# Fused sigmoid attention and low-rank mixing FFN on one core: six pairs' q and k loaded at once, float32 results emptied by VectorE, a new set of planner numbers

## The chip, the cores and the metric

The kernel runs on one core of a Trainium2 chip. The metric is the device time of one execution in microseconds; the median of three runs before the change is 1539.1 us (1538.2 to 1541.37). The engines are named as in the profile: PE (TensorE, matmuls), DVE (VectorE), ACT (ScalarE), POOL (GpSimd) and SP (SyncE, whose queue issues every DMA here).

## The reference, cut to what matters

```python
# q, k, v: (8 batches, 12 heads, 448, 64) float32
scores = q @ k.transpose(0, 1, 3, 2) / sqrt(64) - log(448)
x = (1 / (1 + exp(-scores))) @ v            # -> (8, 448, 768)
xt = x.transpose(0, 2, 1)
u = x + (xt @ U @ V).transpose(0, 2, 1)     # U (448, 32), V (32, 448)
out = u + maximum(u @ w1, 0) @ w2           # w1 (768, 3072), w2 (3072, 768)
```

The weights come to the device as the int64 bits of float64 numbers; the kernel decodes them to float32 itself and splits them into a high and a low float16 part.

## The kernel before, in words

Work is cut by batch. Heads go in pairs (six pairs p in a batch b); two neighbouring pairs, an even and an odd one, form a quad, because the last 64 of 448 rows of both are done together. For each pair `loads` fetches q, k and v, `scores_of` makes scores on PE (L547, and L551 for the last rows), ACT takes the sigmoid (L664), `values_of` multiplies with v (L566, L576), and `out_of` (L703) empties the PSUM bank into one of the six tiles ua or ub of the batch. Batches 0 and 1 (`WHOLE = 2`) do this in float32. The later ones split everything into float16 parts first (the tiles stg, made by POOL and DVE) and their results are scaled when they leave PSUM.

`mix` then does the U and V product for a batch: transposes on PE (L752), copies by ACT (L763), a product with U (L764), a copy (L781), a product with V (L790), an addition by DVE (L792), and `u_parts` splits the result into the float16 tiles us (us__87 for batch 0, us__88 for batch 1). Batch 0 is mixed in two halves, of three tiles each.

The FFN of batches 0 to 3 runs in six groups of w1 and w2 (`ffn_in`, L938; `ffn_out`, L958). In batch 0 each group is decoded on the way: `decode` loads four pieces of int64 bits by SP into one of three w tiles, DVE and ACT turn them into float32 (L401, L404; L453), ACT finds a bound of each piece (L464) and empties the w tile by it, PE spreads the maximum over the partitions (L420), and then the high part (ACT, L908) and the low part (DVE, L404, for example w__90<-stg,s_w__178,w__90) are written and the group is stored in DRAM (kept). Batches 4 to 7 take a form with seven instead of eight products (L1146) from about 958 us on.

The order of the instructions is not written by hand. Every instruction is recorded with an engine, a cost and a place (a number that says how early it is wanted); `Plan.order` then walks a model of the engines and, of the instructions that are ready, issues the one with the least place. The numbers at the top of the file (L59 to L69) set places and the model's costs. Tiles are handed out by the same walk: a ring of buffers has a queue, and a load can be issued when a buffer of its ring is free. The engines run their own lists strictly in order, SP's list of DMA issues too.

Rings that matter here: qk has three buffers (qk__99 to qk__101) for q and k of a pair, v has four (v__102 to v__105). H are the two tiles of the FFN's inner activations (h__93, h__94), unused until the first `ffn_in` of batch 0. The load of q and k is four DMAs of 64 rows for a pair, since each head lies in half of the partitions.

Of the kernel before, what the change touches and what calls it, by code (L numbers as in the profile page):

```python
# [38 lines left out]
P = 128  # L39
D = 64  # L40
# [15 lines left out]
LATER = [2, 4, 3, 5, 6, 7]  # L56
FORMS = {1: (0,), 2: (1,), 3: (2,)}
MM = 0.1893
SWITCH, BOND = 0.11, 6.183  # L59
PIPE, LANDS, LATE = 0.33e6, 3.237, 0.546  # L60

ROOM0, ROOM, AHEAD, BEFORE, PACE = -7.852, 308.311, -53.442, 95.466, 1.111
PREP, BOUNDS, VALUES, SECOND, MIXED = 19.918, -15.21, 0.731, 3.0, 3.524
MIXED1, MIX_1 = 6.837, -10.814
MIX_2, EV_IN, EV_OUT, A_OFF = 34.703, 70.659, 39.745, -7.081
START, DECODE = 63.04, 64.674
U_AT, U_STEP = -3.425, 6.242
LEAD, SUMS, STEP_K, STEP_I, FFN_LEAD = -5.194, 216.012, 10.066, 62.433, 60.97
W_AT, W_STEP, PAIR0, MIX0A, MIX0B, W2_LAG, G0_LEAD = -69.485, 11.668, 3.029, -290.85, -260.87, 0.576, -7.653  # L69
LOW_G = 1  # L70
FB, AB = 8, 0
SHIFT = dict()
# [162 lines left out]
def fused_kernel(ctx: ExitStack, tc: tile.TileContext, q, k, v, wu, wv, w1, w2, out):  # L235
# [12 lines left out]
    def ring(name, n, shape, dtype):  # L248
        return [Buffer(buf(f"{name}{i}_", shape, dtype)) for i in range(n)]
# [194 lines left out]
    def to_f32(words, t, kw, kt, pos, low=False):  # L444

        def lo():
            return words()[:, :, 0]

        def hi():
            return words()[:, :, 1]  # L450

        if low:
            act(0.84, lambda: nc.scalar.activation(  # L453
                t().bitcast(F32), words().bitcast(U16)[:, :, 1], AF.Identity, bias=minus2, scale=-0.936 * 2.0 ** -35), [kw, "minus2"], [kt], pos)
            dve2(0.97, lambda: stt(t(), hi(), 3, t(), ALU.logical_shift_left, ALU.bitwise_or), [kw, kt], [kt], pos)
# [64 lines left out]

    def loads(b, p, early):
        plan.group = f"L{b}{p}"
        qk, v32 = plan.tile("qk", QK), plan.tile("v", V32)
        for h in range(2):
            for i, src in ((1, k), (0, q)):
                load(lambda i=i, h=h: qk.x[rows_of(h), i, :], lambda src=src, h=h: src[b, p, rows_of(h), h, :],
                     D * S * 4, [], [(qk, i, h)], early, cost=0.62)
        load(lambda: v32.x, lambda: v[b, p], P * 512 * 4, [], [(v32, 0), (v32, 1)], early + 0.1)
        mine, other = rows_of(p % 2), rows_of(1 - p % 2)
        load(lambda: v32.x[mine, 3, other], lambda: v[b, p, other, 3, other], D * D * 4, [], [(v32, 1)], early + 0.2)  # L530
        return qk, v32, [(qk, i, h) for i in range(2) for h in range(2)]

    quads = {}

# [48 lines left out]
    def pair(b, p, at, d):  # L583
# [8 lines left out]
        if whole:  # L592
            c, kc = 1.0 / math.sqrt(D), []

            def score_products():
                return [(qk.x[:, 1, :], qk.x[:, 0, :])]

            def value_products():
                return [(v32.x, lambda t, h: t.x[:, h * S : (h + 1) * S])]

            def last_products():
                return [(v32.x[:, 3], lambda t, h: t.x[:, h * S : (h + 1) * S])]

            kscore, kvalue, klast = kqk, [(v32, 0)], [(v32, 1)]
        else:
            prep = at - PREP
            st, sv, ss = plan.tile("stq", STQ), plan.tile("stv", STV), sm("ss", 3)
            v3 = quads[b]["v3"] if odd else plan.tile("v3", V3)
            cm = quads[b]["cm"] if odd else sm("cm", 1)
            mine = rows_of(p % 2)  # L610
            for i in range(2):
                bound(lambda i=i: qk.x[:, i, :], S, lambda i=i: ss.x[:, i : i + 1], kqk[2 * i : 2 * i + 2], (ss, i), prep - BOUNDS, 0.68)
            bound(lambda: v32.x.rearrange("p a b -> p (a b)"), 512, lambda: ss.x[:, 2:3], [(v32, 0), (v32, 1)], (ss, 2), prep - BOUNDS, 0.73)
            s, inv = scale_by_dma(ss, [(ss, i) for i in range(3)], 3, "qkv", prep - BOUNDS + 1)
            cc, cv = sm("c", 1), sm("cv", 1)
            pool(0.3, lambda: ts(nc.gpsimd, cc.x, inv.x[:, 0:1], inv.x[:, 1:2], ALU.mult, 1.0 / math.sqrt(D), ALU.mult), [inv], [cc], prep + 1)
            pool(0.2, lambda: ts(nc.gpsimd, cv.x, inv.x[:, 2:3], 1.0 / A_UP, ALU.mult, 1.0, ALU.mult), [inv], [cv], prep + 1)
            pool(0.2, lambda: ts(nc.gpsimd, cm.x[mine], cc.x[mine], 1.0, ALU.mult, 1.0, ALU.mult), [cc], [(cm, odd)], prep + 1)

            def part(n):  # L620

                n = (2, 3, 1, 0)[n]
                return st.x[:, n * S : (n + 1) * S]

            def parts_v(x):
                return sv.x.rearrange("p (x a b) -> p x a b", x=2, a=3)[:, x]

            def last_v(x):
                return v3.x[:, x * P : (x + 1) * P]

            for i in (1, 0):
                ki = kqk[2 * i : 2 * i + 2]
                pool(0.7, lambda i=i: scaled(part(2 * i), qk.x[:, i, :], s.x[:, i : i + 1]), ki + [s], [(st, 2 * i)], prep + 2,
                     plan.wrote["decoded"])
                dve2(0.68, lambda i=i: rest(part(2 * i + 1), qk.x[:, i, :], s.x[:, i : i + 1], part(2 * i)),
                    ki + [s, (st, 2 * i)], [(st, 2 * i + 1)], prep + 3)
            pool(0.65, lambda: scaled(parts_v(0), v32.x[:, :3], s.x[:, 2:3]), [(v32, 0), s], [(sv, 0)], prep + 6, plan.wrote["decoded"])
            dve2(0.61, lambda: rest(parts_v(1), v32.x[:, :3], s.x[:, 2:3], parts_v(0)), [(v32, 0), s, (sv, 0)], [(sv, 1)], prep + 7)
            pool(0.38, lambda: scaled(last_v(0)[mine], v32.x[mine, 3], s.x[mine, 2:3]), [(v32, 1), s], [(v3, odd, 0)], prep + 7, plan.wrote["decoded"])
# [37 lines left out]
        for j in range(3 + odd):  # L677
# [4 lines left out]
            elif j % 2 == 0:  # L682
                sc = scores_of(b, (j, j + 1) if j == 0 or odd else (j,), products, kj, here, early)
            a = tiles[j] = plan.tile("a2", A2)
            to = a if whole else plan.tile("t2", AT2)
            sigmoid(1.12 if whole else 1.19, lambda to=to: to.x.rearrange("p (h s) -> p h s", h=2),
                    lambda sc=sc, j=j: sc[j].x[:, :, :S], c if j < 3 or whole else cm, here, [sc[j]], [to])
            kto = [to]
            if whole:
# [10 lines left out]
            return  # L700
        for n, (bank, by) in enumerate(((quad["av"], quad["cv"]), (av, None if whole else cv))):
            def out_of(ku=u32[p - 1 + n], bank=bank, by=by, n=n):
                act(0.63, lambda: nc.scalar.activation(ku.x, bank.x[:, :S], AF.Copy, scale=1.0 if whole else by.x),  # L703
                    [bank] + ([] if whole else [by]), [ku], late)
                if b > 0:
                    largest(lambda: ku.x, lambda: mx.x[:, p - 1 + n : p + n], [ku], (mx, p - 1 + n), late)

            out_of()
# [701 lines left out]
```

## Time and profile before

| what | us |
|---|---|
| median of three runs | 1539.1 |
| the profiled execution | 1541.77 |
| its span | 1540.0 |
| PE busy in the span | 1520.0 |
| DVE, ACT, POOL busy | 1110.4, 814.6, 381.9 |
| mean granted TensorE clock | 0.996 of full |

The span runs from the first instruction's start to the last one's end; about 1.8 us of the execution lie outside it. Times in the rows are microseconds from the span's start. In a row of the timeline the first two numbers are start and duration, x is the count of instructions merged in it, and a bracket tells how long the engine was idle before and what ended that. Rows that begin with SPq are DMA issues: the duration is that of the issue and its wait in SP's queue, not of the transfer. In a row of busy time by stretch stand, after the stretch and its length, busy time and instructions of PE, PE's weight loads, DVE, ACT and POOL, then the granted clock, the share of the 16 DMA engines and GB/s. A float32 matmul appears as two records, so "x6" in the order is "x12" in the trace.

### The profile page before, as it was taken

What the parts mean: (1) busy time and instruction counts of PE and PEld (TensorE: products, weight loads), DVE (VectorE), ACT (ScalarE), POOL (GpSimd) and SP (SyncE); (2) the same over time, 40 slices, a digit from 0 to 9 for tenths busy, and PEclk for the clock granted to TensorE, in tenths of its full rate; (3) what the DMA queues carried; (4) which work ended last, traced back from release to release, by engine and by line L of the source; (5) the groups of instructions that cost most, each with busy time, mean ns of one, the idle gap of its engine ahead of it and who ended that gap; (6) DMA issues with size and microseconds to landing.
All of it is one profiled execution on the core that took longest, in us unless ns stands there. A gap on an engine that the chain in (4) does not pass through costs nothing.

```text
span 1540.0 us, 23899 instructions
## 1 busy us (share of the span) xinstructions
PE 1520.0 (99%) x8843; PEld 752.1 (49%) x8843; DVE 1110.4 (72%) x1864; ACT 814.6 (53%) x1327; POOL 381.9 (25%) x538
## 2 busy tenths in 40 slices
PE   8999899999999999999999999999999999999999
PEld 3344455544444444444444444555555555555554
DVE  2788898668878868766678776776867777565656
ACT  5598766478666666666587735332332614131310
POOL 0110001554234462221322540045454500000000
PEclk9899999999999999999999999999999999999999
DMA  7789876675756858555777656866665673443331
GB/s 215 248 300 272 291 260 253 247 257 162 196 156 171 248 180 208 160 158 167 224 217 205 183 213 173 266 216 229 238 233 180 219 251 113 121 126 108 108 108 72
DMA packets 184725, 306.01 MB, mean 199 GB/s; under 512 B 54560, under 2 KB 146080, under 8 KB 178464
## 3 DMA queue, kind: packets, MB, share of 16 engines
q1 hardware_dynamic: 184608, 304.49, 63.5%
q8 instruction: 69, 1.13, 0.3%
q14 instruction: 48, 0.39, 0.1%
HBM read 232.88 MB, written 63.26 MB: 192 GB/s over the span
## 4 chain that ended last, share of the span: by engine, by line
PE 91%; DMA 4%; DVE 2%; ACT 1%; issue 1%; POOL 0%; SPq 0%; ACTq 0%; POOLq 0%
PE banks L1146 37%; PE banks L958 20%; PE banks L938 19%; PE banks L547 6%; PE banks L566 5%; DMA w<-w_in 2%; PE banks L551 1%; PE banks L576 1%; PE banks L848 1%; DMA qk__99<-q_in 1%; DMA qk__99<-k_in 1%; PE banks L858 0%; DVE stg L404 0%; DMA v__104<-v_in 0%; PE banks L790 0%
## 5 line engine op out<-in xcount | busy, mean ns | idle before, releaser
L958 PE MATMUL banks<-h__94,w__92 128*128 128x448 f16 x792 | 157.9, 353 | 4.3 <-DVE xnt L404 3.2
L958 PE MATMUL banks<-h__93,w__91 128*128 128x448 f16 x792 | 157.8, 353 | 0.7 <-ACT h__94 L946 0.7
L404 DVE SCALAR_TENSOR_TENSOR a<-at,a 128x896 f16<-128x896 f32 (+1 forms) x129 | 141.3, 1118 | 14.9 <-ACT a L692 14.5
L938 PEld LDWEIGHTS <-w__90 128*128 128x128 f16 x936 | 91.1, 98 | 88.7 <-issue 5.4
L958 PEld LDWEIGHTS <-w__92 128*128 128x128 f16 x864 | 82.1, 98 | 88.0 <-issue 15.5
L958 PEld LDWEIGHTS <-w__91 128*128 128x128 f16 x864 | 82.0, 98 | 85.8 <-issue 13.0
L1146 PEld LDWEIGHTS <-w__89 128*128 128x128 f16 x819 | 80.1, 98 | 74.8
L1146 PEld LDWEIGHTS <-w__92 128*128 128x128 f16 x819 | 80.1, 98 | 74.7
L1146 PEld LDWEIGHTS <-w__90 128*128 128x128 f16 x819 | 80.1, 98 | 74.6
L692 ACT ACTIVATE a<-at 128x896 f16<-128x896 f32 x126 | 115.3, 950 | 0.6
L938 PEld LDWEIGHTS <-w__89 128*128 128x128 f16 x792 | 77.0, 98 | 74.1 <-issue 3.5
L1002 POOL TENSOR_TENSOR w<-w 128x384 f32<-128x384 f32 x96 | 105.7, 1101 | 4.8
L938 PE MATMUL banks<-us__87,w__90 128*128 128x448 f16 x504 | 99.1, 352 | 2.3 <-ACT h__94 L946 2.3
L938 PE MATMUL banks<-us__88,w__90 128*128 128x448 f16 x432 | 85.5, 353 | 0.0
L938 PE MATMUL banks<-us__88,w__89 128*128 128x448 f16 x432 | 84.8, 353 | 0.0
L1146 PEld LDWEIGHTS <-w__91 128*128 128x128 f16 x567 | 55.5, 98 | 51.8
L998 POOL TENSOR_TENSOR w<-w 128x384 f32<-128x384 f16 x48 | 44.6, 959 | 117.1 <-DVE xnt L1010 82.0
L547 PE MATMUL banks<-stg 64*128 64x448 f16 x648 | 72.7, 351 | 0.0
L938 PE MATMUL banks<-us__87,w__89 128*128 128x448 f16 x360 | 71.1, 353 | 0.0
L566 PE MATMUL banks<-a,stg 128*64 128x448 f16 x648 | 68.2, 355 | 0.0
L945 ACT ACTIVATE r__95<-banks 128x448 f32<-128x448 f32 x48 | 25.9, 539 | 74.2 <-PE banks L938 73.4
L1009 ACT CAST xnt<-w 128x1536 f16<-128x1536 f32 x24 | 35.2, 1468 | 29.4 <-POOL w L1002 29.4
(1119 smaller groups left out, 3068.4 us busy)
## 6 DMA issues: line engine op xcount, KB each, us to landing
w<-w_in SPq DMA_DIRECT2D x48, 768.0 KB, 6.8
forms<-xnt SPq DMA_DIRECT2D x24, 768.0 KB, 4.4
w__89<-kept SPq DMA_DIRECT2D x9, 1536.0 KB, 7.4
w__90<-kept SPq DMA_DIRECT2D x9, 1536.0 KB, 7.2
w__91<-kept SPq DMA_DIRECT2D x9, 1536.0 KB, 8.5
w__92<-kept SPq DMA_DIRECT2D x9, 1536.0 KB, 7.8
w__90<-forms SPq DMA_DIRECT2D x13, 768.0 KB, 5.4
w__89<-forms SPq DMA_DIRECT2D x13, 768.0 KB, 5.8
```

Source lines behind the costliest of these rows:

```text
L404: nc.vector.scalar_tensor_tensor(out=out, in0=in0, scalar=s, in1=in1, op0=op0, op1=op1)
L547: nc.tensor.matmul(sc[j].x[:, h, :S], x[rows_of(h), j * P : j * P + P], y[rows_of(h)], start=i == 0, stop=i == n - 1)
L551: nc.tensor.matmul(sc[j].x[rows_of(m), h, :S], x[rows_of(h), 3 * P : S], y[rows_of(h)], start=i == 0, stop=i == n - 1)
L566: nc.tensor.matmul(av.x[rows_of(h), :S], x[:, j, rows_of(h)], y(tiles[j], h), start=j == 0 and i == 0, stop=not quad and j == 2 and i == n ...
L692: act(0.95, lambda a=a, to=to: nc.scalar.activation(half(a, 0), to.x, AF.Copy, scale=A_UP), kto, [(a, 0)], here + A_OFF)
L938: nc.tensor.matmul(ph.x[:, :S], w.x[:, f, c, x], us.x[:, c, y, :], start=c == 0 and i == 0, stop=c == NP - 1 and i == 2,)
L945: act(0.54, lambda: nc.scalar.activation(r.x, ph.x[:, :S], AF.Relu, scale=DOWN_H), [ph], [r], pos - EV_IN)
L958: nc.tensor.matmul(po.x[:, :S], w.x[:, f, e, x], h.x[:, f, y, :], start=f == 0 and i == 0, stop=f == FC - 1 and i == 2,)
L998: pool(0.93, lambda j=j: nc.gpsimd.tensor_tensor(out=t.x[:, j], in0=quarter(j, 0), in1=quarter(j, 1), op=ALU.add), [w] if b is None else k ...
L1002: pool(1.0, lambda o_=o_, x=x, y=y, sub=sub: nc.gpsimd.tensor_tensor(out=t.x[:, o_], in0=t.x[:, x], in1=t.x[:, y], op=ALU.subtract if sub ...
L1009: act(1.45, lambda: nc.scalar.copy(made(0), t.x.rearrange(order)), [(t, j) for j in range(4)], [(o, 0)], pos)
L1146: nc.tensor.matmul(bank.x[:, :S], wt[1](k, n, x), both(f)[:, y], start=start and k == i == 0, stop=k == 2 and i == 2, skip_group_check=True)
```

## The change

Four things are changed.

1. Batch 0 may take its q and k tiles not only from the three qk buffers but also from four halves of the two H tiles (`QH`).
2. q, and k, of a pair are one DMA of 128 rows each, with an access pattern that takes head 0 for the lower and head 1 for the upper half of the partitions, in place of two DMAs of 64 rows.
3. For batches 0 and 1 the result of a pair leaves PSUM by a copy on VectorE in place of an activation on ScalarE.
4. The planner's numbers, and three of its costs, are others; two lines of that table are shown.

```diff
-SWITCH, BOND = 0.11, 6.183
+SWITCH, BOND = 0.11, 24.665
...
-PREP, BOUNDS, VALUES, SECOND, MIXED = 19.918, -15.21, 0.731, 3.0, 3.524
+PREP, BOUNDS, VALUES, SECOND, MIXED = 6.471, -24.058, 0.174, 3.503, 3.551
...
     QK = ring("qk", 3, [2, S], F32)
+    QH = []
+    for x in H:
+        for i in range(2):
+            t = Buffer(x.ap.rearrange("p f x s -> p (f x s)")[:, 4 * i * S : 4 * (i + 1) * S].bitcast(F32).rearrange("p (x s) -> p x s", x=2))
+            t.shares.append(x)
+            x.shares.append(t)
+            QH.append(t)
...
-        qk, v32 = plan.tile("qk", QK), plan.tile("v", V32)
-        for h in range(2):
-            for i, src in ((1, k), (0, q)):
-                load(lambda i=i, h=h: qk.x[rows_of(h), i, :], lambda src=src, h=h: src[b, p, rows_of(h), h, :],
-                     D * S * 4, [], [(qk, i, h)], early, cost=0.62)
+        qk, v32 = plan.tile("qk", QK + QH if b == 0 else QK), plan.tile("v", V32)
+
+        def own(src):
+            x = src[b, p]
+            return bass.AP(x.tensor, x.offset, [[D * 2 * S + S, 2], [2 * S, D], [1, S]])
+
+        for i, src in ((1, k), (0, q)):
+            load(lambda i=i: qk.x[:, i, :], lambda src=src: own(src), P * S * 4, [], [(qk, i)], early)
...
             def out_of(ku=u32[p - 1 + n], bank=bank, by=by, n=n):
-                act(0.63, lambda: nc.scalar.activation(ku.x, bank.x[:, :S], AF.Copy, scale=1.0 if whole else by.x),
-                    [bank] + ([] if whole else [by]), [ku], late)
+                if whole:
+                    dve(0.6, lambda: nc.vector.tensor_copy(ku.x, bank.x[:, :S]), [bank], [ku], late)
+                else:
+                    act(0.63, lambda: nc.scalar.activation(ku.x, bank.x[:, :S], AF.Copy, scale=by.x), [bank, by], [ku], late)
```

Three places of the order show what moved. The lines of the new file stand 7 (in the helpers), 10 or 12 below those of the old one: L378 is L385, L404 is L411, L464 is L471, L763 is L775, L664 is L674.

SP's queue between the third and the fourth piece of the first weight group, before. w_in are weight pieces, v_in is v, and the qk rows load pairs 3 and 4 of batch 0:

```order
L378 DMA v__105<-v_in 64x64
L378 DMA qk__99<-k_in 64x448
L378 DMA qk__99<-q_in 64x448
L378 DMA qk__99<-k_in 64x448
L378 DMA qk__99<-q_in 64x448
L378 DMA qk__100<-k_in 64x448
L378 DMA qk__100<-q_in 64x448
L378 DMA qk__100<-k_in 64x448
L378 DMA qk__100<-q_in 64x448
L378 DMA v__102<-v_in 128x512
L378 DMA v__103<-v_in 128x512
L378 DMA w_107<-w_in 128x6x128
```

The same place now; h__94 holds q and k of pair 5 of batch 0, and the qk rows here are pairs 0 and 1 of batch 1:

```order
L385 DMA h__94<-k_in 128x1x448
L385 DMA h__94<-q_in 128x1x448
L385 DMA w_107<-w_in 128x6x128
L385 DMA v__105<-v_in 64x64
L385 DMA w_107<-w_in 128x6x128 x2
L385 DMA qk__99<-k_in 128x1x448
L385 DMA qk__99<-q_in 128x1x448
L385 DMA qk__100<-k_in 128x1x448
L385 DMA qk__100<-q_in 128x1x448
L385 DMA v__102<-v_in 128x512
L385 DMA v__103<-v_in 128x512
L385 DMA w_107<-w_in 128x6x128
```

All of batch 0's q and k now stand ahead of the first weight piece; before, pairs 3 to 5 stood behind it. Ahead of the fourth piece there are six issues after the third, before there were twelve.

DVE's list at the fourth weight piece, before. uraw and vraw are U and V being decoded, stg is the weight piece:

```order
L401 TENSOR_SCALAR stg<-w_107 128x768
L401 TENSOR_SCALAR uraw<-w_107 128x128
L404 SCALAR_TENSOR_TENSOR stg<-w_107,stg 128x768
L404 SCALAR_TENSOR_TENSOR uraw<-w_107,uraw 128x128
L404 SCALAR_TENSOR_TENSOR stg<-w_107,stg 128x768
L404 SCALAR_TENSOR_TENSOR uraw<-w_107,uraw 128x128
```

The same place now; ua__77 and ua__78 are the results of pairs 2 and 3 of batch 0:

```order
L408 TENSOR_SCALAR stg<-w_107 128x768
L411 SCALAR_TENSOR_TENSOR stg<-w_107,stg 128x768 x2
L408 TENSOR_SCALAR uraw<-w_107 128x128
L714 COPY ua__77<-banks 128x448
L714 COPY ua__78<-banks 128x448
L880 TENSOR_REDUCE mm_w__167<-ssw__164 128x1
L411 SCALAR_TENSOR_TENSOR uraw<-w_107,uraw 128x128 x2
```

The two results stand between the first and the second step of U.

ACT's list around the second half of batch 0's mixing, before. xnt rows are the four copies of transposed results, w_107,ssw rows are bounds of decoded weight pieces:

```order
L763 COPY xnt<-banks 128x384
L664 ACTIVATE a<-banks,bias_s 128x896
L763 COPY xnt<-banks 128x384
L464 ACTIVATE w_107,ssw__165<-at 128x768
L763 COPY xnt<-banks 128x384
L464 ACTIVATE w_107,ssw__165<-at 128x768
L464 ACTIVATE w_107,ssw__165<-us__88 128x768
L763 COPY xnt<-banks 64x384
```

The same place now (L460 is L453, the first step of a decoding):

```order
L775 COPY xnt<-banks 128x384
L460 ACTIVATE us__88<-w_107,minus_65 128x768
L775 COPY xnt<-banks 128x384
L471 ACTIVATE w_107,ssw__165<-at 128x768
L471 ACTIVATE w_107,ssw__165<-us__88 128x768
L775 COPY xnt<-banks 128x384
L775 COPY xnt<-banks 64x384
```

One bound more has moved ahead of the first copy, and a decoding step of the next group stands between the first and the second.

More of the change, by code (lines that the diff above doesn't have):

```diff
@@ L58 @@
 MM = 0.1893
-SWITCH, BOND = 0.11, 6.183
-PIPE, LANDS, LATE = 0.33e6, 3.237, 0.546
-ROOM0, ROOM, AHEAD, BEFORE, PACE = -7.852, 308.311, -53.442, 95.466, 1.111
-PREP, BOUNDS, VALUES, SECOND, MIXED = 19.918, -15.21, 0.731, 3.0, 3.524
[L64 to L69, printed above, removed]
+SWITCH, BOND = 0.11, 24.665
+PIPE, LANDS, LATE = 0.33e6, 3.237, 0.625
+ROOM0, ROOM, AHEAD, BEFORE, PACE = -9.538, 305.553, -56.066, 102.147, 1.089
+PREP, BOUNDS, VALUES, SECOND, MIXED = 6.471, -24.058, 0.174, 3.503, 3.551
+MIXED1, MIX_1 = 7.164, -39.064
+MIX_2, EV_IN, EV_OUT, A_OFF = 13.189, 93.613, 38.047, -2.03
+START, DECODE = 66.062, 61.784
+U_AT, U_STEP = 2.925, 2.333
+LEAD, SUMS, STEP_K, STEP_I, FFN_LEAD = -54.33, 232.637, 33.074, 120.231, 39.636
+W_AT, W_STEP, PAIR0, MIX0A, MIX0B, W2_LAG, G0_LEAD = -64.044, 6.75, 4.33, -370.163, -300.635, 0.622, -6.831
 LOW_G = 1
@@ L452, in to_f32 @@
         if low:
-            act(0.84, lambda: nc.scalar.activation(
+            act(0.99, lambda: nc.scalar.activation(
                 t().bitcast(F32), words().bitcast(U16)[:, :, 1], AF.Identity, bias=minus2, scale=-0.936 * 2.0 ** -35), [kw, "minus2"], [kt], pos)
@@ L530, in loads @@
         load(lambda: v32.x[mine, 3, other], lambda: v[b, p, other, 3, other], D * D * 4, [], [(v32, 1)], early + 0.2)
-        return qk, v32, [(qk, i, h) for i in range(2) for h in range(2)]
+        return qk, v32, [(qk, i) for i in range(2)]
     quads = {}
@@ L611, in pair @@
             for i in range(2):
-                bound(lambda i=i: qk.x[:, i, :], S, lambda i=i: ss.x[:, i : i + 1], kqk[2 * i : 2 * i + 2], (ss, i), prep - BOUNDS, 0.68)
+                bound(lambda i=i: qk.x[:, i, :], S, lambda i=i: ss.x[:, i : i + 1], kqk[i : i + 1], (ss, i), prep - BOUNDS, 0.68)
             bound(lambda: v32.x.rearrange("p a b -> p (a b)"), 512, lambda: ss.x[:, 2:3], [(v32, 0), (v32, 1)], (ss, 2), prep - BOUNDS, 0.73)
@@ L631, in pair @@
             for i in (1, 0):
-                ki = kqk[2 * i : 2 * i + 2]
+                ki = kqk[i : i + 1]
                 pool(0.7, lambda i=i: scaled(part(2 * i), qk.x[:, i, :], s.x[:, i : i + 1]), ki + [s], [(st, 2 * i)], prep + 2,
@@ L685, in pair @@
             to = a if whole else plan.tile("t2", AT2)
-            sigmoid(1.12 if whole else 1.19, lambda to=to: to.x.rearrange("p (h s) -> p h s", h=2),
+            sigmoid(1.0 if whole else 1.09, lambda to=to: to.x.rearrange("p (h s) -> p h s", h=2),
                     lambda sc=sc, j=j: sc[j].x[:, :, :S], c if j < 3 or whole else cm, here, [sc[j]], [to])
```

## The prediction

> **What bounds the kernel now.** I read the page's first part, then busy time and granted clock by stretch, then who TensorE (PE) waited for, then the timelines of the places that these name.
>
> ```profile
> span 1540.0 us, 23899 instructions
> PE 1520.0 (99%) x8843; PEld 752.1 (49%) x8843; DVE 1110.4 (72%) x1864; ACT 814.6 (53%) x1327; POOL 381.9 (25%) x538
> ```
>
> PE works 99% of the span. The stretches show where the rest is lost (columns: length, then busy us and instructions of each engine, granted clock, DMA share, GB/s):
>
> ```profile
> 8.80:23.50 14.70, 14.70 (x80) 5.34 (x76) 4.90 (x6) 11.19 (x16) 0.00 (x0) 1.00 0.92 254
> 23.50:25.90 2.40, 0.04 (x1) 0.04 (x1) 0.78 (x2) 0.88 (x2) 0.00 (x0) 1.00 0.40 99
> 25.90:29.40 3.50, 3.50 (x9) 2.95 (x11) 1.69 (x2) 1.74 (x3) 0.00 (x0) 0.51 0.71 188
> 63.40:67.20 3.80, 1.71 (x9) 0.29 (x5) 1.71 (x3) 2.86 (x7) 0.00 (x0) 0.96 0.98 349
> 67.20:77.20 10.00, 10.00 (x24) 3.55 (x26) 8.44 (x15) 6.36 (x9) 0.52 (x1) 0.50 0.56 180
> 100.00:140.00 40.00, 40.00 (x212) 17.82 (x210) 32.52 (x57) 37.50 (x63) 0.00 (x0) 1.00 0.91 304
> 160.00:180.00 20.00, 15.74 (x92) 9.09 (x91) 16.26 (x32) 14.45 (x28) 1.32 (x4) 1.00 0.72 250
> 180.00:240.00 60.00, 57.73 (x310) 30.06 (x309) 59.13 (x111) 44.77 (x76) 2.87 (x7) 1.00 0.84 295
> 240.00:290.00 50.00, 50.00 (x267) 26.04 (x266) 41.46 (x66) 29.69 (x48) 9.67 (x9) 1.00 0.57 220
> ```
>
> Three things cost time, all before 200 us. A: PE stands from 23.5 to 25.9 and then runs at half clock for 3.5 us. B: gaps near 65 us, then 10 us at half clock. C: 4.3 us idle in 160 to 180 and 2.3 in 180 to 240. VectorE (DVE) is busy 59.13 of 60 us in 180 to 240; ScalarE (ACT) 37.50 of 40 in 100 to 140. The names come from PE's waits (us in total, times, longest):
>
> ```profile
> PE banks L547 <- DMA qk__99<-q_in: 6.6, 2, 4.2
> PE banks L958 <- DVE xnt L404: 3.2, 1, 3.2
> PE banks L938 <- ACT h__94 L946: 2.3, 1, 2.3
> PE banks L764 <- ACT xnt L763: 1.5, 1, 1.5
> PE banks L958 <- DVE e_w__170 L423: 1.1, 1, 1.1
> PE banks L790 <- ACT xnt L781: 0.6, 1, 0.6
> ```
>
> The first row is the start (4.2) and A (2.4); L764 and L790 are B; L958 and L938 are C, 6.6 us together, waits for a PSUM bank that DVE or ACT has not emptied. So the kernel is bound by PE's work, and only what PE loses early can be won.
>
> Own time against the median: the profiled execution took 1541.77 us, 1540.0 of it span; the median of the three runs, 1539.1, lies 2.7 lower. I sum on the profiled one and move the result down by 2.7.
>
> **Part 1: q and k of pairs 3 to 5 in the FFN tiles (term A).** Rows of PE's timeline, of the chain of waits (twelve score matmuls, twelve value matmuls) and of SyncE (SP), whose queue issues the loads:
>
> ```profile
> 25.86 4.46 PE L547 MATMUL banks<-qk__99 64*128 64x448 f32 x12 [2.37 <-DMA qk__99<-q_in]
> 31.24 2.46 PE banks L547 x12
> 33.69 2.40 PE banks L566 x12
> 13.81 3.20 SPq L378 DMA_DIRECT2D v__104<-v_in  x1
> 17.78 0.59 SPq L378 DMA_DIRECT2D qk__99<-k_in  x1
> 28.02 1.11 SPq L378 DMA_DIRECT2D w<-w_in  x1
> 40.53 1.33 SPq L378 DMA_DIRECT2D w<-w_in  x3
> ```
>
> Pair 3 takes the place of pair 0 in qk__99, and its loads are issued only at 17.78, behind a 3.20 us wait of SP's queue and behind three weight pieces; PE waits 2.37 us. The twelve matmuls after that take 4.46 us where the same twelve at full clock took 2.46, so half clock costs 2.0 here; by the clock row it is 3.5 x 0.49 = 1.7. In the new order pair 3 goes to h__93, ahead of the weights, with nothing to wait for. Term: -(2.37 + 1.7) = -4.1. The loads keep ahead of PE: a pair's q, k and v are 0.74 MB, the stretch 8.8 to 23.5 moves 254 GB/s, so a pair lands every 2.9 us, while PE takes 2.46 + 2.40 = 4.9 for its scores and values alone.
>
> The skill weighs against the second half of this term: by "TensorE: Matmul & The Clock Gate", section "What's actually happening", the clock falls after an idle window of about 3.4 us. By that alone a gap of 2.37 would leave it up, and the term were -2.4. The trace does not agree: the clock was 0.51 right after that gap.
>
> What may stand there instead: the first mixing needs ua__77 and ua__78, which DVE now copies, and in its order they stand behind the decoding of U, whose load is behind a 64x64 piece of v that waits for a landing. Nobody but PE waits for these two copies; behind them on DVE stand the rest of U and V. I take +1.0, between 0 (hidden behind the values of pair 4, which stand just ahead) and +2.4 (as long as the gap removed).
>
> **One transfer each.** SP issues 96 fewer, of about 0.6 us (17.78: 0.59). The first score needs two whole tiles now instead of two halves; it may start up to 0.6 later, but its second head no longer waits for issues three and four. I take 0, between -1 and +0.6. Later this shortens SP's queue by 1.2 us a pair in front of weight pieces; it counts in the decoding below.
>
> **Part 2: results through VectorE.** Twelve copies of 128x448 leave ACT and go to DVE. The nearest rows (ns, min/median/max):
>
> ```profile
> L703 ACT ACTIVATE ua__75<-banks x1: 522/522/522, 21.8 to 21.8; 128x448 f32<-128x448 f32 x1
> L703 ACT ACTIVATE ub__86<-banks x1: 538/538/538, 142.6 to 142.6; 128x448 f32<-128x448 f32 x1
> L792 DVE TENSOR_TENSOR ua__75<-banks,ua__75 x1: 625/625/625, 51.1 to 51.1; 128x448 f32<-128x448 f32 x1
> ```
>
> ACT loses 12 x 0.53 = 6.4 us. No copy out of PSUM by DVE is in the trace; the add that reads the same shape from a bank takes 0.62, ACT's own 0.53, so 12 x 0.53 to 0.62 = 6.4 to 7.4; I take the add, the nearer in engine: 7.4. Six of them fall before 65 us. Cover: in 8.8 to 23.5 DVE is busy 4.9 of 14.7 us. The other six stand near 80, 106 and 142, where ACT is the fuller one (37.50 against 32.52 of 40). So on PE's path I cost them at nothing; without that cover the last six cost 3.7 us of decoding.
>
> **Part 3: places anew (terms B and C).** B hangs on ACT's queue:
>
> ```profile
> 64.38 0.84 ACT L464 ACTIVATE w<-us__88 128x768 bf16<-128x768 f32 x1 [0.92 <-DVE us__88 L404]
> 65.23 0.46 ACT L763 COPY xnt<-banks 64x384 f32<-64x384 f32 x1
> 67.12 4.84 PE L790 MATMUL banks<-vraw,xnt 32*128 32x448 f32 x6 [0.56 <-ACT xnt L781]
> ```
>
> The fourth copy of the second mixing half waits behind the bound of a weight piece that DVE has not decoded. In the new order copies three and four still stand behind two such bounds, but the later pieces come sooner. (The first three come later: 1.4 MB of q and k more stand ahead of them, 5.4 us at 254 GB/s; DVE has little else there, and a group's scale needs the fourth anyway.) The fourth was issued at 28.02; between it and the third stood twelve other issues and now stand six, 6 x 0.59 = 3.5 us less. Ahead of the next three (40.53) fall away as many again, 7 in all; those also wait for buffers that ACT empties, so I put them 4.5 us sooner, between 3.5 and 7. B is worth 1.5 + 0.6 + 10.0 x 0.5 = 7.1 in all. I take half, -3.5, between 0 and -7.1.
>
> C: PE now reaches the decode-paced stage about 6.6 us sooner, with DVE and ACT as full as before. Banks may then be waited for longer, or, with weights sooner, not at all. I take 0, between -6.6 and +6.6. What limits how far PE may run ahead is the last two decoded groups:
>
> ```profile
> 256.74 1.94 DVE L404 SCALAR_TENSOR_TENSOR w__90<-at,s_w__177,w__90 128x768 f16<-128x768 f32 x2
> 260.48 3.76 PE L938 MATMUL banks<-us__87,w__90 128*128 128x448 f16 x19
> 284.28 1.94 DVE L404 SCALAR_TENSOR_TENSOR w__92<-at,s_w__178,w__92 128x768 f16<-128x768 f32 x2
> 290.10 2.24 PE L958 MATMUL banks<-h__94,w__92 128*128 128x448 f16 x11
> ```
>
> Group 5's first quarter is ready at 256.74 + 0.97 = 257.7 and used at 260.48: 2.8 us ahead. Its second weight is ready at 286.2 and used at 290.10: 3.9 ahead. A gain over 2.8 us holds only if the decoding, too, ends that much sooner; for -6.6 it needs 3.8, less than the 4.5 us by which the early pieces come sooner.
>
> After 290 us nothing in the change shortens PE's work: the same matmuls in other places.
>
> Sum: -4.1 + 1.0 + 0 + 0 - 3.5 + 0 = -6.6, so 1535.2 for an execution like the profiled one, 1532.5 for the median.
>
> **The rivals.**
> *Given back at the decoding.* The early microseconds are won, but DVE and ACT decode no faster, and PE waits for group 5. Then the gain is the 2.8 us of slack: 1539.1 - 2.8 = 1536.3. For it: DVE's 59.13 of 60. Against: DVE has room where the pieces come sooner (4.9 busy of 14.7).
> *VectorE becomes the bound: slower.* Place: the decoding from 80 to 260 us, on DVE's list, which is served in order; each copy stands ahead of decoding and may wait there for PE's values. If the sooner pieces bring DVE nothing, its list through group 5 grows by the 7.4 us of copies; PE used that group 2.8 us after it was ready, so it is 4.6 later: 1539.1 + 4.6 = 1543.7. It decides from where the sooner pieces bring DVE less than 4.6 us. For it: 59.13 of 60 busy. Against: 4.5 us sooner pieces, and six of the copies stand where DVE has room.
> *All of it goes.* B and a good part of C vanish: -4.1 + 1.0 - 7.1 - 3 = -13.2: 1525.9. For it: every one of these waits is a queue's order, which is what was set anew. Against: DVE's load.
> *The change doesn't do what it says:* SP's order with its rows of h__94, and no load of pairs 3 to 5 into a qk tile, excludes that.
>
> **How the numbers follow.** Forecast 0.50, given back 0.20, slower 0.10, all of it 0.20. The runs of before spread over 3 us, so a difference under 0.2% (3.1 us) can't be told from none. Faster than 1536.0: the forecast, all of it, and a quarter of the case given back, 0.75. Same: the rest of that, 0.15. Slower: 0.10. The range 1525.5 to 1539.5 holds the forecast, the case given back and the upper half of the last one; it leaves out the slower case and the far end.
>
> **What would show it.** Right: no gap of PE near 23.5 us and full clock there; copies of about 0.6 us on DVE's list; less idle and less half clock near 60 to 75; group 5's first matmul at about 254. Wrong: the gap of A comes back within 10 us (waiting for U or for v of pair 4); or PE's idle in 140 to 300 grows by more than 4 us; or that first matmul stands at 258 or later; or PE shows gaps after 300.

## The result, and the profile after

The changed kernel takes 1805.8 us (median of 4, 1804.2 to 1807.5) against 1540.2 us (4 runs, 1538.2 to 1541.4): a ratio of 1.173 (1.171 to 1.175), 266 us slower. The forecast was 1532.5, range 1525.5 to 1539.5.

The page's first rows after (span 1805.2; before 1540.0):

```profile
span 1805.2 us, 23735 instructions
PE 1580.5 (88%) x8843; PEld 766.8 (42%) x8843; DVE 1121.0 (62%) x1876; ACT 806.8 (45%) x1315; POOL 395.5 (22%) x538
PEclk9688889999888989999988989999999999999999
```

The same 8843 matmuls keep PE busy 60.5 us longer, because the clock falls again and again (its mean is 0.939 in place of 0.996), and PE stands idle for 224.7 us instead of 20.0. DVE, ACT and POOL are busy within 14 us of before, far from the span, so none of them has become the bound. Busy time by stretch, as in the prediction, with the share of the DMA engines and GB/s at the end:

```profile
8.00:15.00 7.00, 1.98 (x6) 1.25 (x8) 0.00 (x0) 0.02 (x1) 0.00 (x0) 1.00 0.13 49
60.00:150.00 90.00, 55.65 (x229) 20.10 (x229) 48.56 (x94) 38.09 (x59) 6.62 (x8) 0.77 0.47 153
150.00:300.00 150.00, 115.13 (x570) 53.72 (x571) 97.43 (x178) 88.60 (x152) 5.77 (x14) 0.87 0.67 228
450.00:600.00 150.00, 113.70 (x724) 52.48 (x725) 88.86 (x158) 77.77 (x131) 40.64 (x65) 0.87 0.43 112
800.00:960.00 160.00, 136.07 (x849) 64.55 (x848) 94.12 (x173) 83.45 (x140) 30.82 (x69) 0.93 0.46 145
1140.00:1500.00 360.00, 360.00 (x2015) 184.09 (x2012) 265.56 (x410) 145.43 (x225) 143.34 (x146) 1.00 0.67 216
```

And the first of these stretches in the kernel before:

```profile
8.00:15.00 7.00, 7.00 (x38) 2.90 (x34) 0.00 (x0) 6.36 (x7) 0.00 (x0) 1.00 0.75 222
```

PE lacks work throughout the part of the program that loads q and k, and is full in the last stretch, which loads none. In 8 to 15 us, when little but q and k is on its way, 49 GB/s move and the DMA engines are busy 0.13 of the time: 2 of 16 is 0.125. The rows of SP's queue after show what one such load takes, since an issue there waits until the queue takes it (start, duration):

```profile
4.79 0.54 SPq L385 DMA_DIRECT2D qk__100<-k_in  x1
5.37 4.62 SPq L385 DMA_DIRECT2D qk__100<-q_in  x1
10.03 4.55 SPq L385 DMA_DIRECT2D v__103<-v_in  x1
14.62 0.54 SPq L385 DMA_DIRECT2D qk__101<-k_in  x1
15.20 4.63 SPq L385 DMA_DIRECT2D qk__101<-q_in  x1
...
50.07 4.24 SPq L385 DMA_DIRECT2D w<-w_in  x1
```

A load of q or k is 128 x 448 x 4 bytes = 0.229 MB; at 49 GB/s that is 4.7 us, the 4.6 of these rows. A pair needs two, 9.3 us, while PE takes 4.9 for its scores and values. The first weight piece is issued at 50.07, behind all of batch 0's q and k. The packets themselves are not slower: for the same 304.5 MB they take, by part 3 of the page, 52.6% of 16 engines' span here, 950 us, and 63.5% before, 978 us. Two rows tell who waits: PE's first row, and the longest wait for the loads of q over the whole span (us in total, times):

```profile
13.02 4.85 PE L557 MATMUL banks<-qk__99 64*128 64x448 f32 x12 [13.02 <-DMA qk__99<-q_in]
```
```profile
  ACT junk L471: 175.1, 31
```

The first score stands at 13.0 us (before 4.2). In the later batches ScalarE, which takes the bound of each pair's q, waits 175 us for q to land.

### The profile page after: what moved, and what is told of

It is laid out like the page before. It is cut to its first block, busy times and chain, and to the rows that moved or that the text cites. A ratio compares the mean times of both kernels' runs of the same rounds, so it can differ in the third digit from the quotient of the medians.

```text
span 1805.2 us, 23735 instructions
## 1 busy us (share of the span) xinstructions
PE 1580.5 (88%) x8843; PEld 766.8 (42%) x8843; DVE 1121.0 (62%) x1876; ACT 806.8 (45%) x1315; POOL 395.5 (22%) x538
## 3 DMA queue, kind: packets, MB, share of 16 engines
q1 hardware_dynamic: 181728, 304.48, 52.6%
## 4 chain that ended last, share of the span: by engine, by line
PE 42%; DMA 5%; ACT 1%; DVE 1%; issue 1%; SPq 0%; ACTq 0%; DVEq 0%
PE banks L1158 32%; PE banks L970 4%; PE banks L950 3%; DMA qk__100<-q_in 2%; DMA qk__99<-q_in 2%; PE banks L557 1%; PE banks L576 1%; DMA qk__101<-q_in 1%; DMA w<-parked 1%; DMA qk__100<-k_in 0%; PE banks L860 0%; ACT at L674 0%; PE banks L561 0%; DVE stg L411 0%; PE banks L586 0%
## 5 line engine op out<-in xcount | busy, mean ns | idle before, releaser
L970 PE MATMUL banks<-h__94,w__92 128*128 128x448 f16 x864 | 181.9, 366 | 13.1 <-ACT h__94 L958 7.2
L970 PE MATMUL banks<-h__93,w__91 128*128 128x448 f16 x864 | 178.0, 360 | 8.2 <-ACT ub__85 L716 7.6
L411 DVE SCALAR_TENSOR_TENSOR a<-at,a 128x896 f16<-128x896 f32 (+1 forms) x129 | 143.5, 1128 | 66.3 <-ACT a L702 66.2
L950 PEld LDWEIGHTS <-w__90 128*128 128x128 f16 x936 | 91.5, 99 | 92.5 <-issue 11.6
L970 PEld LDWEIGHTS <-w__92 128*128 128x128 f16 x864 | 85.1, 101 | 104.0 <-issue 35.2
L970 PEld LDWEIGHTS <-w__91 128*128 128x128 f16 x864 | 83.7, 99 | 97.9 <-issue 27.5
L557 PE MATMUL banks<-stg 64*128 64x448 f16 x648 | 79.8, 372 | 50.4 <-ACT at L674 37.9
L950 PEld LDWEIGHTS <-w__89 128*128 128x128 f16 x792 | 80.3, 102 | 90.0 <-issue 26.1
L1158 PEld LDWEIGHTS <-w__91 128*128 128x128 f16 x819 | 80.1, 98 | 74.8
L1158 PEld LDWEIGHTS <-w__90 128*128 128x128 f16 x819 | 80.1, 98 | 74.8
L1158 PEld LDWEIGHTS <-w__89 128*128 128x128 f16 x819 | 80.1, 98 | 74.5
L950 PE MATMUL banks<-us__87,w__90 128*128 128x448 f16 x504 | 100.7, 357 | 3.0 <-ACT h__93 L958 3.0
L576 PE MATMUL banks<-a,stg 128*64 128x448 f16 x648 | 72.4, 364 | 26.1 <-ACT a L702 16.9
L950 PE MATMUL banks<-us__88,w__89 128*128 128x448 f16 x432 | 86.8, 357 | 3.5 <-ACT at L674 2.2
L950 PE MATMUL banks<-us__88,w__90 128*128 128x448 f16 x432 | 87.2, 357 | 0.0
L950 PE MATMUL banks<-us__87,w__89 128*128 128x448 f16 x360 | 81.4, 387 | 2.3 <-ACT at L674 1.6
L1158 PEld LDWEIGHTS <-w__92 128*128 128x128 f16 x567 | 55.5, 98 | 51.8
L557 PEld LDWEIGHTS <-stg 64*128 64x128 f16 x648 | 28.1, 97 | 94.3 <-issue 76.7
L411 DVE SCALAR_TENSOR_TENSOR stg<-w,stg 128x768 int32<-128x768 int32 x48 | 44.8, 951 | 29.2 <-ACT stg L460 29.0
```

The costliest lines, as they stand in the source:

```text
L411: nc.vector.scalar_tensor_tensor(out=out, in0=in0, scalar=s, in1=in1, op0=op0, op1=op1)
L557: nc.tensor.matmul(sc[j].x[:, h, :S], x[rows_of(h), j * P : j * P + P], y[rows_of(h)], start=i == 0, stop=i == n - 1)
L576: nc.tensor.matmul(av.x[rows_of(h), :S], x[:, j, rows_of(h)], y(tiles[j], h), start=j == 0 and i == 0, stop=not quad and j == 2 and i == n ...
L950: nc.tensor.matmul(ph.x[:, :S], w.x[:, f, c, x], us.x[:, c, y, :], start=c == 0 and i == 0, stop=c == NP - 1 and i == 2,)
L970: nc.tensor.matmul(po.x[:, :S], w.x[:, f, e, x], h.x[:, f, y, :], start=f == 0 and i == 0, stop=f == FC - 1 and i == 2,)
L1158: nc.tensor.matmul(bank.x[:, :S], wt[1](k, n, x), both(f)[:, y], start=start and k == i == 0, stop=k == 2 and i == 2, skip_group_check=True)
```

## The experiments

**The change with a pattern that begins with 128.** If few engines are the cause, it is enough to change the pattern, and the host's layout of the rows with it.

```diff
-        def own(src):
-            x = src[b, p]
-            return bass.AP(x.tensor, x.offset, [[D * 2 * S + S, 2], [2 * S, D], [1, S]])
...
-            load(lambda i=i: qk.x[:, i, :], lambda src=src: own(src), P * S * 4, [], [(qk, i)], early)
+            load(lambda i=i: qk.x[:, i, :], lambda src=src: src[b, p, :, 0, :], P * S * 4, [], [(qk, i)], early)
...
-        return np.ascontiguousarray(np.concatenate([x, x], axis=2))
+        return np.ascontiguousarray(np.concatenate([x, x[:, :, :, ::-1]], axis=2))
```

> The changed kernel with its order of instructions untouched. Only the source pattern of the one-transfer load differs: the host lays head 1 of q and k where row 64+d of the first column is read, so that the pattern counts 128 rows in one step instead of 2 heads times 64 rows. Bytes, transfers, places and copies are the same. Theory (few engines): a transfer whose pattern begins with a count of 2 is worked off by 2 of the 16 DMA engines (the DMA share is 0.13 at 49 GB/s in 8 to 15 us), 4.5 us apiece; with 128 in front it is spread over all. Then the loss of 265 us goes as a whole and the time is 1525 to 1540, my blind sum giving 1532.5; the stretch 8 to 15 us moves over 200 GB/s. Rival (places): the new order, with all q and k ahead of the weights and VectorE's copies in the list, is what starves PE; the time stays at 1800 or so. Rival (one big transfer): a single transfer of 224 KB that must land whole is late as such; the time stays over 1700.

Measured: 1532.3 us (1530.9 to 1533.1) beside 1543.0 of the kernel before, ratio 0.992 (0.991 to 0.994). Its stretches, to be held against the two of 8 to 15 us above and those of the prediction:

```profile
2.00:8.00 6.00, 3.88 (x11) 2.01 (x13) 0.00 (x0) 1.92 (x2) 0.00 (x0) 1.00 0.92 302
8.00:15.00 7.00, 7.00 (x40) 2.77 (x38) 0.00 (x0) 5.23 (x7) 0.00 (x0) 1.00 0.95 312
25.90:29.40 3.50, 2.80 (x16) 0.90 (x12) 1.84 (x3) 3.50 (x6) 0.00 (x0) 1.00 1.02 343
67.20:77.20 10.00, 9.70 (x51) 3.30 (x50) 9.86 (x21) 9.89 (x17) 1.86 (x3) 1.00 0.85 262
155.60:159.00 3.40, 2.80 (x8) 1.16 (x8) 3.40 (x6) 2.53 (x5) 0.00 (x0) 0.50 0.85 177
```

With loads of the same size 302 to 312 GB/s now move, and the whole loss is gone: 273.5 us by the pattern alone. Both rivals fall: the places and the size of the transfer are unchanged here.

**The change with four loads.** The lines that name the halves of a tile are left out.

```diff
...
-        for i, src in ((1, k), (0, q)):
-            load(lambda i=i: qk.x[:, i, :], lambda src=src: own(src), P * S * 4, [], [(qk, i)], early)
+        for h in range(2):
+            for i, src in ((1, k), (0, q)):
+                load(lambda i=i, h=h: qk.x[rows_of(h), i, :], lambda src=src, h=h: src[b, p, rows_of(h), h, :],
+                     D * S * 4, [], [(qk, i, h)], early, cost=0.62)
...
```

> The changed kernel with four loads of 64 rows for a pair, as before the change, and all else of the change kept (the FFN tiles for q and k, VectorE's copies, the new numbers); the planner walks anew with 96 issues more, so the order differs in detail from that of the changed kernel. Few engines: the loss goes, 1528 to 1550, a few us worse than with one well-spread transfer, since the numbers were not set for this order. Places: about 1800.

Measured: 1567.3 us, ratio 1.015 (1.013 to 1.017). The big loss is gone, but 35 us over the spread run is more than expected. Here two things differ, the issues and the order that the planner makes with them; a run below parts them.

**Counts of 2 and 4 in the kernel before, at even steps.** The case with 2; the other has 4 in place of 2.

```diff
+        def own(src, h):
+            x = src[b, p, rows_of(h), h, :]
+            return bass.AP(x.tensor, x.offset, [[2 * S * (D // 2), 2], [2 * S, D // 2], [1, S]])
...
```

> The kernel before, its order untouched, four loads of 64 rows for a pair as it has them, same addresses and bytes; only the source pattern is written as 2 times 32 rows instead of 64. Few engines: each load takes 32 packets on each of two engines, about 2.3 us, 192 loads 434 us on those two, as in the changed kernel; they also carry a sixteenth of all else (DMA share 0.64 of 1540 us), so PE starves in the same stages: 1700 to 1850. Rivals (places; one big transfer): nothing of theirs is in this kernel, 1538 to 1542.

> As the one before, but written as 4 times 16 rows. Few engines: 4 engines, 16 packets each, 1.1 us a load, 217 us on each of the four beside their sixteenth of all else. From 300 to 960 us a pair comes every 21 us or so, in which an engine has 14 us of other work and 4.5 us of this: it fits, so only the start and the first two batches lose, 4.5 us a pair against 4.9 us of PE's own: 1545 to 1600. If time went with the engines' work alone, half of the loss of the case with two. Rivals: 1538 to 1542.

Measured: 1543.2 and 1545.7 us, ratios 1.000 (0.998 to 1.001) and 1.001 (0.999 to 1.003). Taken at their word these runs would refute the theory. But the traffic is that of the kernel before; the stretch of the case with 2:

```profile
8.00:15.00 7.00, 7.00 (x29) 4.18 (x26) 0.00 (x0) 6.12 (x7) 0.00 (x0) 1.00 0.70 218
```

Two axes whose steps fit together are joined to one of 64 rows when the kernel is built: the built loads read 64x448 as before, where those of the changed kernel have an axis more, 128x1x448. The experiment had not made what it was to test, and says nothing on the theory, although 1545.7 lies in the range expected of the case with 4.

**Counts that can't be joined.** Rows 32 to 63 now come from the second copy of the data, so that the step between the halves differs.

```diff
+        def own(src, h):
+            x = src[b, p, 0, h, :]
+            return bass.AP(x.tensor, x.offset, [[2 * S * 96, 2], [2 * S, 32], [1, S]])
...
-                load(lambda i=i, h=h: qk.x[rows_of(h), i, :], lambda src=src, h=h: src[b, p, rows_of(h), h, :],
+                load(lambda i=i, h=h: qk.x[rows_of(h), i, :], lambda src=src, h=h: own(src, h),
```

> The kernel before, its order untouched, four loads of 64 rows for a pair. The two tries with 2 times 32 and 4 times 16 rows showed the DMA traffic of the kernel before (218 and 228 GB/s in 8 to 15 us, before 222), so a pattern with one even step counts as 64 rows however it is written. Here the two halves can't be joined: every row d of q and k lies twice in memory, and rows 32 to 63 are read from the second copy, so the pattern counts 2 times 32 rows with different steps. Same bytes, same destination. Few engines: 32 packets on each of 2 engines, 2.3 us a load, 192 loads; DMA share about 0.13 at 8 to 15 us, and PE starves as in the changed kernel: 1700 to 1850. Rivals (places; one big transfer): 1538 to 1545.

> As the one before, with 4 times 16 rows that can't be joined (the host lays the rows four times). Few engines: 4 engines, 1.1 us a load, DMA share about 0.25 at 8 to 15 us; a pair takes 4.5 us of those four against 4.9 us of PE's own in the first batches, and from 300 to 960 us an engine has 14 + 4.5 us of work for a pair every 21 us: it fits. So it loses at the start and a little in the first two batches: 1545 to 1600, far less than half of the case with 2. Rivals: 1538 to 1545.

> As the one before, with 8 times 8 rows (laid eight times). Few engines: 8 engines, 0.57 us a load, as long as its issue (0.59 us), so SP's issuing covers it: 1538 to 1555. Any extra cost of a pattern with one axis more, whatever its count, would show here too, as a time far over 1555.

Measured: 1817.2, 1595.9 and 1542.3 us, ratios 1.181 (1.179 to 1.183), 1.037 (1.035 to 1.039) and 1.002 (1.001 to 1.003), with the order, the bytes and the number of loads of the kernel before (for 4 and 8 the step of 96 rows is 80 and 72, and the host lays the rows four and eight times). Stretches in which almost nothing but q and k moves, with 2, 4 and 8 in front:

```profile
8.00:15.00 7.00, 3.69 (x8) 1.63 (x10) 0.00 (x0) 0.00 (x0) 0.00 (x0) 1.00 0.13 49
```
```profile
27.00:29.00 2.00, 2.00 (x12) 0.57 (x8) 1.93 (x3) 1.72 (x4) 0.00 (x0) 1.00 0.27 94
```
```profile
22.20:24.40 2.20, 2.20 (x18) 0.77 (x18) 2.13 (x4) 1.12 (x3) 0.00 (x0) 1.00 0.54 191
```

The share of the engines and the traffic double with the count: 0.13, 0.27 and 0.54, beside 2, 4 and 8 of 16. (In 8 to 15 us the case with 4 shows 0.43 and not the 0.25 expected, since v goes there too.) So the count in front makes the loss, in a kernel that has nothing else of the change; and as the case with 8 has an axis more too and loses hardly anything, it is the count and not the axis. The loss is far from proportional: 278, 57 and 3.5 us for 2, 4 and 8. All three times lie within their ranges, the second at its upper end. The 3.5 us are no more than what two sets of runs of the kernel before differ by (1538.8 and 1543.0).

**Two loads of 64 rows at the place of the one.**

```diff
-        def own(src):
-            x = src[b, p]
-            return bass.AP(x.tensor, x.offset, [[D * 2 * S + S, 2], [2 * S, D], [1, S]])
+        def both(i, src):
+            for h in range(2):
+                nc.sync.dma_start(out=qk.x[rows_of(h), i, :], in_=src[b, p, rows_of(h), h, :])
...
         for i, src in ((1, k), (0, q)):
-            load(lambda i=i: qk.x[:, i, :], lambda src=src: own(src), P * S * 4, [], [(qk, i)], early)
+            dma(0.42, P * S * 4, lambda i=i, src=src: both(i, src), [], [(qk, i)], early)
```

> The changed kernel with its order untouched (FFN tiles, VectorE's copies, new places), but each load of q or k is issued as two transfers of 64 rows, one behind the other at the place where the one stands. Few engines: every transfer is spread again, so the loss goes without a change of the host's layout: 1531 to 1540; 0 to 8 us over the 1532.3 of the run with 128 rows, for 96 issues of 0.6 us on SP's queue, of which the two ahead of the first score count on PE's path. The run with four loads planned anew (1567) would then have lost by its order and not by its issues; if this run too stands near 1567, the issues themselves cost it. Places, or one big transfer: the latter as here, the former 1800.

Measured: 1544.1 us, ratio 1.004 (1.003 to 1.006): the FFN tiles, VectorE's copies and the new places, without fewer issues, are 0.4% slower than before. It is 11.8 us over the run with 128 rows, or 18 by the two ratios, since the kernel before took 1538.8 beside this one and 1543.0 beside the other; more than the 0 to 8 expected. Against the run with the same loads planned anew (1567.3, ratio 1.015) that is 17 us less by the ratios and 23 by the medians: this much of that run's loss was its order. Here a gap stands again where A stood, and one at the first mixing:

```profile
28.71 2.31 PE L557 MATMUL banks<-h__93 64*128 64x448 f32 x4 [3.65 <-DVE ua__75 L714]
44.71 0.33 PE L764 MATMUL banks<-ident,ua__77 128*128 128x128 f32 x1 [1.18 <-DVE ua__77 L714]
```

The first gap is not A's wait. Pair 3 lies in h__93, whose loads go out in time; PE waits for the bank that VectorE's copy of ua__75 empties. That copy stands in VectorE's list behind the first weight piece, and with twelve issues more ahead of it this piece goes out 8 us later than in the run with 128 rows. Here, from SP's queue and VectorE's timeline:

```profile
11.80 1.23 SPq L534 DMA_DIRECT2D h__93<-q_in  x2
19.96 0.60 SPq L385 DMA_DIRECT2D w<-w_in  x1
26.57 0.56 DVE L408 TENSOR_SCALAR stg<-w 128x768 int32<-128x768 int32 x1 [26.57 <-DMA w<-w_in]
28.05 0.61 DVE L714 COPY ua__75<-banks 128x448 f32<-128x448 f32 x1
```

And in the run with 128 rows:

```profile
11.60 0.61 SPq L385 DMA_DIRECT2D w<-w_in  x1
21.08 0.62 DVE L710 COPY ua__75<-banks 128x448 f32<-128x448 f32 x1
```

**One spread transfer, and nothing else of the change.** The host lays the rows as in the run with 128 rows.

```diff
-                load(lambda i=i, h=h: qk.x[rows_of(h), i, :], lambda src=src, h=h: src[b, p, rows_of(h), h, :],
-                     D * S * 4, [], [(qk, i, h)], early, cost=0.62)
+                def one(i=i, h=h, src=src):
+                    if not h:
+                        nc.sync.dma_start(out=qk.x[:, i, :], in_=src[b, p, :, 0, :])
+                dma(0.62, D * S * 4, one, [], [(qk, i, h)], early)
```

> The kernel before, its order untouched (no FFN tiles, no VectorE copies, its own numbers), but q and k of a pair each come by one transfer of 128 rows, laid so that 16 engines share it, at the place where head 0 was loaded; the loads of head 1 fall away: 96 issues fewer. Theory (the issues carry the gain): the run in place with 96 issues more lost all that the change wins, +11.8 us, within the first 100 us; so fewer issues alone bring most of the gain here: 1528 to 1534, and the stretch 2 to 8 us moves 300 GB/s in place of 204. Rival (the places carry it): pair 3 still waits for qk__99 behind v, A and B stay, and only some tenths are won: 1536 to 1541. My own step, which put the one-transfer form at 0 (between -1 and +0.6), would say 1538 to 1540.

Measured: 1532.1 us (1531.4 to 1535.1) beside 1542.3, ratio 0.994 (0.993 to 0.996). The kernel before, in its own order, has the full gain. Its queue, its first stretch and the place of A:

```profile
0.72 0.39 SPq L528 DMA_DIRECT2D qk__99<-k_in  x1
1.17 0.42 SPq L528 DMA_DIRECT2D qk__99<-q_in  x1
1.64 0.42 SPq L378 DMA_DIRECT2D v__102<-v_in  x1
...
14.58 0.53 SPq L528 DMA_DIRECT2D qk__99<-k_in  x1
```
```profile
2.00:8.00 6.00, 3.95 (x12) 2.09 (x14) 0.00 (x0) 1.99 (x2) 0.00 (x0) 1.00 0.89 300
23.50:25.90 2.40, 2.40 (x18) 0.79 (x14) 0.00 (x0) 2.40 (x5) 0.00 (x0) 1.00 0.71 184
63.40:67.20 3.80, 3.80 (x15) 1.04 (x16) 3.80 (x10) 2.06 (x4) 0.53 (x1) 0.55 0.58 192
```

Pair 3 still takes qk__99 behind v and three weight pieces, but is issued at 14.58 instead of 17.78, and PE does not wait for it. My step that put the one-transfer form at 0 is refuted, and so is the rival that the places carry the gain.

**The copies back on ScalarE.** The diff is against the run with 128 rows.

```diff
-                    dve(0.6, lambda: nc.vector.tensor_copy(ku.x, bank.x[:, :S]), [bank], [ku], late)
+                    dve(0.6, lambda: nc.scalar.activation(ku.x, bank.x[:, :S], AF.Copy, scale=1.0), [bank], [ku], late)
```

> The changed kernel with the well-spread 128-row transfer (1532.3 us), the order otherwise untouched, but the 12 results of batches 0 and 1 leave PSUM by an activation on ScalarE again, each at the same point of the program. VectorE is rid of 12 x 0.62 = 7.4 us, ScalarE gets 12 x 0.53 = 6.4 us. My step (the copies are covered on either engine): 1530 to 1535. Rival (the move to VectorE carries part of the gain, since ScalarE is the fuller engine while the two batches are made): 1536 to 1542. The other way round (the copies cost VectorE's decoding up to 3.7 us): 1528 to 1530.

Measured: 1532.4 us (1530.8 to 1532.8), ratio 0.994 (0.992 to 0.995), beside the same runs of before as the previous one. With spread transfers the engine of the copies makes no difference that shows.

**A count of 2 in some batches only.** In the run with 128 rows, where b < WHOLE (the other run: b >= WHOLE); the loads then read own(src):

```diff
+        def own(src):
+            x = src[b, p]
+            if b < WHOLE:
+                return bass.AP(x.tensor, x.offset, [[S, 2], [2 * S, D], [1, S]])
+            return x[:, 0, :]
```

> The changed kernel with the 128-row transfer, the order untouched, but the 24 loads of batches 0 and 1 have a pattern that begins with 2 again (head 0 from the first column, head 1 from the second). Few engines: by 190 us the changed kernel lay 113 us behind the run with 128 rows, and by 300 us still 113, so this part alone costs about 113: 1630 to 1660. The 24 loads alone keep two engines 24 x 4.5 = 108 us.

> As the one before, the other way round: the 72 loads of batches 2 to 7 begin with 2, those of batches 0 and 1 are spread. Few engines: from 300 to 900 us the changed kernel fell back by another 161 us: 1670 to 1710. If the two parts do not add up to the whole loss of 273 us over the spread run (the sum far under it), the late weights of the first part and not the engines' work alone make the later one.

Measured: 1626.4 and 1723.1 us, 94 and 191 us over the 1532.3 of the spread run. Together they make 285, the whole loss 273.5, so they add up to within 11 us: the later part does not hang on the first. They miss their ranges by 4 and 13 us.

## Why the prediction was wrong, step by step

**One transfer each** is the step that failed: "I take 0, between -1 and +0.6". It counted issues and asked when the first score may start, and took the speed of the transfers from rows of other patterns: "a pair's q, k and v are 0.74 MB, the stretch 8.8 to 23.5 moves 254 GB/s". The changed pattern moved 49 GB/s. That it begins with a count of 2 stood in the diff; the diff was read for how many issues fall away and not for how the remaining ones are worked off. No row of before showed such a pattern, so its price should have been bounded by far rows, both ways; I gave it a width of 1.6 us. Measured, it is +273.5 us as written, and when spread -10 us on the kernel before, and on the changed one -12 by the medians or -18 by the ratios.

The rule stands in the Trainium skill: "DMA: Bandwidth & Descriptors", section "Why a DMA increments its semaphore by 16 and not by 1", which says that a transfer uses the largest number of engines up to 16 that divides the slowest dimension of both its patterns. By that the change's loads run on 2 engines. The traces agree: with 2, 4 and 8 in front the share of the engines is 0.13, 0.27 and 0.54 and the traffic 49, 94 and 191 GB/s, and with 128 it is 0.92 and 302 GB/s.

**The FFN tiles (A, -4.1).** In the run with 128 rows A is 0.70 us of gap and no half clock:

```profile
28.53 1.02 PE L553 MATMUL banks<-h__93 64*128 64x448 f32 x4 [0.70 <-ACT a L670]
```

That is -3.4, near the size forecast. But the tiles are not needed for it: either of two things removes pair 3's wait. With the tiles, in the changed order, its loads go out at 10 to 13 us even with four issues a pair; without the tiles, but with two issues, they go out at 14.58; in neither run does PE wait for them. What the prediction did not see is that a late weight piece brings a gap back at the same place, by way of VectorE's copies.

**The wait at the first mixing (+1.0).** With fewer issues it does not come; with four it is there as described, 1.18 us for ua__77 behind DVE's copies.

**VectorE's copies (0).** Right where the loads are spread: 1532.3 with them, 1532.4 without. Each takes 0.60 to 0.62, forecast 0.62:

```profile
L710 DVE COPY ua__75<-banks x1: 617/617/617, 21.1 to 21.1; 128x448 f32<-128x448 f32 x1
```

Where the weight pieces come late it does not hold, since the copies stand behind them in VectorE's list. With four issues PE waits 3.65 and 1.18 us for copies, and in the changed kernel 16.4 and 10.3 us for the same two (us in total, times, longest):

```profile
PE banks L557 <- DVE ua__75 L714: 16.4, 1, 16.4
PE banks L764 <- DVE ua__77 L714: 10.3, 1, 10.3
```

They are a way by which the slow loads reach PE, not a cause of their own: the kernel before, with its copies on ScalarE, lost 278 us to a count of 2 as well.

**B (-3.5) and C (0).** The timeline of PE in the run with 128 rows, the gaps that are left up to 160 us:

```profile
58.64 1.59 PE L772 MATMUL banks<-xnt,uraw 128*32 128x384 f32 x4 [0.89 <-ACT xnt L771]
67.50 1.02 PE L553 MATMUL banks<-qk__101 64*128 64x448 f32 x4 [0.30 <-ACT a L670]
118.81 2.43 PE L966 MATMUL banks<-h__93,w__91 128*128 128x448 f16 x12 [1.64 <-ACT a L670]
156.20 3.80 PE L966 MATMUL banks<-h__94,w__92 128*128 128x448 f16 x12 [4.60 <-DVE ua__76 L411]
```

B: 1.2 us of 7.1 remain, -5.9. C: 1.64 + 4.60, and 2.8 us at half clock behind the longer one (156.2 to 159.0), 1.4: 7.6 in place of 6.6, +1.0. In 290 to 1525 us PE is full, where 1.15 us were lost before (1233.85 of 1235):

```profile
290.00:1525.00 1235.00, 1235.00 (x7395) 617.86 (x7393) 877.80 (x1452) 604.96 (x990) 340.51 (x479) 1.00 0.59 183
```

So the spread run's sum is -3.4 - 5.9 + 1.0 - 1.15 = -9.4 (before rounding) against -6.6 forecast, and its profiled execution took 1532.29 against 1541.77, -9.5. That its median falls on my 1532.5 is luck: A, B, C, the mixing and the end were missed by 0.7, 2.4, 1.0, 1.0 and 1.15 us, and beside its own runs of the kernel before it gains 10.7 us, not 6.6.

**After 290 us.** That "nothing in the change shortens PE's work" held, but the later batches' loads have the same form, and they cost most: 191 of 285 us. I had followed the change only through the first batches.

**The rivals.** None named the transfer's own speed. The slower one, VectorE as the bound, did not happen: DVE is busy 62% after, and PE's waits for its copies begin with weights that VectorE itself waits for. The case that "the change doesn't do what it says" was put aside by SP's order, and an order shows where a transfer stands, not how long it takes.

What stays open: why the four-load form planned anew lost 17 to 23 us by its order; only that it did is shown. Its first weight pieces are issued at 27.07 us, against 19.96 with two loads in place, but no run parts this from the rest of its order.

## What to carry to other kernels

Before two transfers are made one, look at the count with which each pattern begins, once axes that fit together are joined: at 2 the same bytes came at 49 GB/s, at 128 at over 300. Where the layout is yours, lay the data so that one step runs over all partitions; that alone, in the kernel before, gave 1532.1 us, as much as all of the change with it, and both kernels are beaten by it. An edit whose operation the trace has never shown gets a wide range, however small it looks in the diff.

## What the runs showed of the hardware that was not expected

For the first pair a load of 128 rows was issued in 0.39 and 0.42 us, one of 64 rows in 0.58 to 0.60; later ones spread wider. The first load of v, of 128 rows in both kernels, went from 0.59 to 0.42 when its neighbours changed, so the rows alone do not set the time. Two loads in place of four took 0.8 us of SP's time for the first pair instead of 2.4, and the first microseconds moved 300 GB/s instead of 204.

The clock fell after short gaps, and not at once. In the kernel before with spread transfers two gaps of about half a microsecond end at 59.64 and 61.03; the clock stayed full until 63.4 and was at half from 64 to 66, while PE was busy:

```profile
59.64 0.83 PE L766 MATMUL banks<-xnt,uraw 64*32 64x384 f32 x2 [0.53 <-ACT xnt L765]
61.03 2.52 PE L792 MATMUL banks<-vraw,xnt 32*128 32x448 f32 x6 [0.56 <-ACT xnt L783]
62.00:63.00 1.00, 1.00 (x4) 0.44 (x3) 0.92 (x2) 0.13 (x1) 0.00 (x0) 1.00 0.73 205
64.00:65.00 1.00, 1.00 (x4) 0.00 (x0) 1.00 (x3) 0.70 (x2) 0.14 (x1) 0.50 0.49 173
```

Nor does the length of a gap alone tell. In the kernel before, the clock was 0.51 behind the 2.37 us of A, but stayed full behind a gap of 3.19 us, where twelve matmuls took the 2.43 us that they take at full clock:

```profile
174.18 2.43 PE L958 MATMUL banks<-h__94,w__92 128*128 128x448 f16 x12 [3.19 <-DVE xnt L404]
```

No run here shows what decides it: the gaps alone, when they fall, or the small matmuls (32 rows or columns of the array) around them.
